# Attention followed by routed experts: separate expert buffers, moved transposes, a later row table and filler matmuls

## The chip, the cores and the metric

The kernel runs on one core of one Trainium2 chip. The metric is the device time of one execution in microseconds (us); three runs of the kernel before gave 316.18, 316.77 and 318.23. The core has five engines that this text names: TensorE (PE in the profile, PEld for its weight loads), VectorE (DVE), ScalarE (ACT), GpSimd (POOL) and SyncE (SP). They run at the same time and wait for each other by semaphores. TensorE writes only to PSUM, the accumulation memory[...].

## What is computed

Block-wise causal attention for 8 batches, 8 heads, 576 tokens and 64 values a head, followed by a mixture of 8 experts. A token's expert is found from its id alone.

```python
scores = scale * q @ k.T                      # 576 x 576 for each batch and head
mask   = block_i >= block_j                   # blocks of 64 tokens
attn   = exp(where(mask, scores, -1e9) - max); attn /= sum(attn)
x      = (attn @ v) -> rows (4608, 512)       # one row for each token
expert = token_ids * 2654435761 % 8           # the factor is 1 modulo 8, so: the low three bits of the id
for e in range(8):
    out[expert == e] = relu(x[expert == e] @ w1[e]) @ w2[e]   # 512 -> 1024 -> 512
```

## The kernel before

The kernel has two stages. **Attention** works through 32 pairs of heads (4 pairs a batch), numbered g = 0 to 31. For one pair, three chunks of scores (`S_chunk`) are computed into PSUM tiles of pool `psS`, of which there are two; ScalarE takes the exp of each chunk into `pt`. The outputs (`PV`) of a pair are computed one turn later, into the single PSUM tile `O`, and VectorE divides by the row sums (`norm`) into `xs`. After each batch, `xs` is written to a table of rows in device memory, `x_dram`.

Queries and keys arrive with tokens on the partitions and must be transposed first. `T_group(b, n)` is a quarter of that for batch b: 18 transposes on TensorE into one PSUM tile, and one VectorE copy into `qT` or `kT`.

```python
def S_chunk(g, ch):
    ps = psS.tile([P, 2, 512], F32, tag="ps")            # two buffers
    for n, (o0, kt, q0, w) in enumerate(CHUNKS[ch]):
        mm_pair(b, pr, ps, o0, kt, q0, w, first=n == 0)   # L172
    for o0 in MASKS[ch]:
        mm_mask(ps, o0, ...)                              # L182
    nc.scalar.activation(ptv[...], ps[:], ACT.Exp, scale=SCALE)   # L200

def T_group(b, n, pool=None):
    if b not in qkTs:
        qkTs[b] = [att.tile([P, NP, S], BF16, name=x, tag=x, bufs=3) for x in ("qT", "kT")]
    ...
    for c in range(n):
        for m in range(2):
            nc.tensor.transpose(...)                      # L159
    copy(qkTs[b][w]..., tp[...])                          # L164, VectorE
```

Beside this, VectorE, GpSimd and TensorE build the **row table**: which token stands in which slot of which expert. `route()` computes the slots in steps (`next(rgen)` runs the next step), and `place_a`, `place_p`, `place_b`, `place_c` enter one batch at a time: comparisons on VectorE (L387, L391), products on GpSimd, five matmuls on TensorE (L411), an addition on VectorE. `placed` ends it.

The turn of one pair, with the lists that say what goes where:

```python
for n in range(WARM):                                     # WARM = 40
    nc.tensor.matmul(warm[:, 0, 0:P], ...)
rgen = route(); next(rgen)
load_qk(0); load_v(0); load_qk(1); load_v(1)
T_group(0, 2); T_group(0, 3, pool=(psO, "O")); T_group(0, 0, pool=(psS, "ps")); T_group(0, 1, pool=(psS, "ps"))

for g in range(NPAIRS + 1):
    S_chunk(g, 0); S_chunk(g, 1)
    for bn in Ts[g, 0]: T_group(*bn)       # between scores and outputs
    if g >= 1:
        PV(g - 1, 0); PV(g - 1, 1)          # L237, L242
        if g in mids: pq = place_b(mids[g], g - 1)
        norm(g - 1)                         # L254, L255
        if g in mids: place_c(pq)
    S_chunk(g, 2)
    if pr == 0: S_rest(b)                   # a small fourth chunk, once a batch
    for bn in Ts[g, 1]: T_group(*bn)       # behind the third chunk
    for step in steps[g]: step()
    ...                                     # write_x, gathers, loads
att_ctx.close()                             # the attention pools end here
mx = ctx.enter_context(tc.tile_pool(name="mx", bufs=2))   # xT and hT of the experts
```

The **expert stage** gathers the rows of an expert from `x_dram` (128 rows a tile, `gather_x`, L463, on GpSimd), transposes them on TensorE (L561) with a copy to `xT` by VectorE (L562), multiplies by w1 with a relu on ScalarE into `hT` (L574, L579; for the first two experts in parts, L593, L597), multiplies by w2 (L607) and scatters the rows to the output (L614). The first three tiles of experts 0 and 1 are gathered already during attention, since they hold only rows of batches 0 to 5.

Of the kernel before, what the change touches and what calls it, by code (L numbers as in the profile page):

```python
# [10 lines left out]
F32 = mybir.dt.float32  # L11
BF16 = mybir.dt.bfloat16
# [7 lines left out]
B, H, S, D = 8, 8, 576, 64  # L20
RUN = 18
DV = 96
NV = 4
E, DM, FF = 8, 512, 1024
N = B * S
NT = 4
NP = H // 2
# [4 lines left out]
GA = EARLY // 128  # L32
OVT = 32
NG = E * G + OVT
WARM = 40
NEG = -30000.0
SCALE = 1.0 / float(D) ** 0.5

# [2 lines left out]
def kernel(  # L41
# [10 lines left out]
    nc = tc.nc  # L52
    P = nc.NUM_PARTITIONS

    const = ctx.enter_context(tc.tile_pool(name="const", bufs=1))
    dram = ctx.enter_context(tc.tile_pool(name="dram", bufs=1, space=bass.MemoryType.DRAM))
    wts = ctx.enter_context(tc.tile_pool(name="wts", bufs=2))

    x_dram = dram.tile([N, DM], BF16, name="x_dram")

# [6 lines left out]
    onesbf = const.tile([P, P], BF16, name="onesbf")  # L67
# [5 lines left out]
    inc = const.tile([P, E], F32, name="inc")  # L73

    nc.vector.memset(onesbf[:], 1.0)
    nc.gpsimd.iota(jmp[:], pattern=[[1, P]], base=0, channel_multiplier=-1,
                   allow_small_or_imprecise_dtypes=True)
    nc.vector.tensor_single_scalar(identbf[:], jmp[:], 0.0, op=ALU.is_equal)
    nc.vector.tensor_single_scalar(lower[:], jmp[:], 0.0, op=ALU.is_gt)

    nc.vector.memset(maskk[:], 0.0)
    nc.vector.memset(maskq[:], 0.0)
    for m in range(2):
# [4 lines left out]
    psS = att_ctx.enter_context(tc.tile_pool(name="psS", bufs=2, space=bass.MemoryType.PSUM))  # L88
    psT = att_ctx.enter_context(tc.tile_pool(name="psT", bufs=1, space=bass.MemoryType.PSUM))
    psO = att_ctx.enter_context(tc.tile_pool(name="psO", bufs=1, space=bass.MemoryType.PSUM))  # L90
    ld = att_ctx.enter_context(tc.tile_pool(name="ld", bufs=2))
    fix = att_ctx.enter_context(tc.tile_pool(name="fix", bufs=1))
    att = att_ctx.enter_context(tc.tile_pool(name="att", bufs=2))
# [53 lines left out]
    qkTs = {}  # L147


    def T_group(b, n, pool=None):  # L150
        if b not in qkTs:
            qkTs[b] = [att.tile([P, NP, S], BF16, name=x, tag=x, bufs=3) for x in ("qT", "kT")]
        w, z = divmod(n, 2)
        c0, n = RUN // 2 * z, RUN // 2
        pool, tag = pool or (psT, "tp")
        tp = pool.tile([P, 16, P], BF16, name="tp", tag=tag)
        for c in range(n):
            for m in range(2):
                nc.tensor.transpose(out=tp[64 * m : 64 * m + 64, c, :],  # L159
                                    in_=loaded[b][w][:, m, c0 + c, :], identity=identbf[:])  # L160
        parts = ((nc.vector.tensor_copy, 0, P),) if b > 0 else (
            (nc.vector.tensor_copy, 0, 64), (nc.scalar.copy, 64, P))
        for copy, r0, r1 in parts:
            copy(qkTs[b][w][:].rearrange("p r (j c) -> p (r j) c", c=RUN)[:, r0:r1, c0 : c0 + n],  # L164
                 tp[:, 0:n, r0:r1].rearrange("p c r -> p r c"))
# [25 lines left out]
    def S_chunk(g, ch):  # L191
        b, pr = divmod(g, NP)
        ps = psS.tile([P, 2, 512], F32, name="ps", tag="ps")
# [3 lines that stand above are left out]
            mm_mask(ps, o0, last=o0 == MASKS[ch][-1])  # L197
        pt = pts[g % 2]
        ptv = pt[:, 0 : 2 * PTW].rearrange("p (m n) -> p m n", m=2)
        nc.scalar.activation(ptv[:, :, 512 * ch : 512 * ch + 512], ps[:], ACT.Exp, scale=SCALE)  # L200

    def S_rest(b):
        qT, kT = qkTs[b]
        ps = psS.tile([P, 2, 512], F32, name="ps", tag="ps")
        for pr in range(NP):
            for m in range(2):
                rows = slice(64 * m, 64 * m + 64)
                nc.tensor.matmul(
                    ps[rows, 0, 64 * pr : 64 * pr + 64],
                    lhsT=kT[rows, pr, 512:576], rhs=qT[rows, pr, 512:576],  # L210
                    start=(pr == 0), stop=(pr == NP - 1),
                )
        nc.scalar.activation(pt4s[b % 2][:, 0 : NP * 64], ps[:, 0, 0 : NP * 64], ACT.Exp, scale=SCALE)
# [63 lines left out]
    def route():  # L277
# [2 lines left out]
        nc.vector.tensor_single_scalar(ei[:], lo[:, :, 0], E - 1, op=ALU.bitwise_and)  # L280
        eb = rt.tile([B, S], BF16, name="eb")
        nc.vector.tensor_copy(eb[:], ei[:])
        pr = psT.tile([P, 5, 65], F32, name="pr", tag="tp")
        for i in range(5):
            n = P if i < NT else 64
            nc.tensor.matmul(pr[0:n, i, 0:B], lhsT=eb[:, 128 * i : 128 * i + n],
                             rhs=identbf[0:B, 0:B], start=True, stop=True)
# [59 lines left out]
        for z, sl in ((0, slice(0, 5 * BA)), (1, slice(5 * BA, T))):  # L347
            n = sl.stop - sl.start
# [35 lines left out]
    def place_a(b):  # L384
        ohp = rt.tile([P, 5, P], BF16, name="ohp", tag="ohp", bufs=2)
        ohg = rt.tile([P, 5, 2, NG], BF16, name="ohg", tag="ohg", bufs=2)
        nc.vector.tensor_tensor(  # L387
            out=ohp[:], in0=iota_p[:, None, :].to_broadcast([P, 5, P]),
            in1=slo[:, b, :, None].to_broadcast([P, 5, P]), op=ALU.is_equal)
        ohs = rt.tile([P, 5, NG], BF16, name="ohs", tag="ohs", bufs=2)  # L390
        nc.vector.tensor_tensor(  # L391
            out=ohs[:], in0=iota_p[:, None, 0:NG].to_broadcast([P, 5, NG]),
            in1=shi[:, b, :, None].to_broadcast([P, 5, NG]), op=ALU.is_equal)
        places[b] = (ohp, ohg, ohs)

    def place_p(b):
        ohp, ohg, ohs = places[b]
        nc.gpsimd.tensor_tensor(
            out=ohg[:, :, 0, :], in0=ohs[:],
            in1=vhi[:, b, :, None].to_broadcast([P, 5, NG]), op=ALU.mult)  # L400
        nc.gpsimd.tensor_tensor(
            out=ohg[:, :, 1, :], in0=ohs[:],
            in1=vlo[:, :, None].to_broadcast([P, 5, NG]), op=ALU.mult)


    def place_b(b, g):
        ohp, ohg, _ = places.pop(b)
        pq = ots[g][:, 0, 512 - 2 * NG :]
        for i in range(5):
            n = P if i < NT else 64  # L410
            nc.tensor.matmul(pq, lhsT=ohp[0:n, i, :],  # L411
                             rhs=ohg[0:n, i, :, :].rearrange("p w g -> p (w g)"),
                             start=(i == 0), stop=(i == 4))
        return pq
# [60 lines left out]
    rgen = route()  # L475
# [3 lines left out]
    load_qk(1)  # L479
    load_v(1)  # L480
    T_group(0, 2)
    T_group(0, 3, pool=(psO, "O"))
    T_group(0, 0, pool=(psS, "ps"))
    T_group(0, 1, pool=(psS, "ps"))

    Ts = {(g, z): [] for g in range(NPAIRS + 1) for z in range(2)}
    for b in range(1, B):
        at = {1: ((1, 1), (2, 0), (2, 1), (3, 0)), 2: ((4, 1), (5, 1), (6, 0), (6, 1))}.get(
            b, tuple((4 * b - 5 + z, 1) for z in range(4)))
        for n, gz in zip((2, 3, 0, 1), at):  # L490
            Ts[gz].append((b, n))
    steps = {g: [] for g in range(NPAIRS + 1)}
# [3 lines left out]
    steps[4] += [lambda: next(rgen, None), rows]  # L496
    mids = {}
    for j in range(B):
        steps[5 + 2 * j].append(lambda j=j: place_a(j))
        steps[6 + 2 * j].insert(0, lambda j=j: place_p(j))  # L500
        mids[9 + 2 * j] = j
    steps[24].append(placed)
    loads = {g: [] for g in range(NPAIRS + 1)}
    for b, g in enumerate((1, 4, 7, 10, 13, 16), 2):
        loads[g].append((load_qk, b))
        loads[g + 1 if b > 2 else 3].append((load_v, b))
    for g, what in ((19, (load_w1, 0)), (21, (load_w1, 1)), (22, (load_w2, 0)), (29, (load_w2, 1))):
        loads[g].append(what)
    for g in range(NPAIRS + 1):
        b, pr = divmod(g, NP)  # L510
        live = g < NPAIRS
        if live:
            S_chunk(g, 0)
            S_chunk(g, 1)
        for bn in Ts[g, 0]:
            T_group(*bn)
        if g >= 1:
            PV(g - 1, 0)
            PV(g - 1, 1)
            if g in mids:  # L520
                pq = place_b(mids[g], g - 1)
            norm(g - 1)
            if g in mids:
                place_c(pq)
        if live:
            S_chunk(g, 2)
            if pr == 0:
                S_rest(b)
        for bn in Ts[g, 1]:
            T_group(*bn)  # L530
        for step in steps[g]:
            step()
        if pr == 0 and b >= 1:
            write_x(b - 1)
        if 12 <= g < 12 + 2 * G:
            nc.gpsimd.memset(xgs[g - 12][:], 0.0)
        if g in (28, 29):
            gather_x(g - 28, 0, GA)
        for load, n in loads[g]:
            load(n)  # L540
    att_ctx.close()


    mx = ctx.enter_context(tc.tile_pool(name="mx", bufs=2))
    mo = ctx.enter_context(tc.tile_pool(name="mo", bufs=8))
    psH = ctx.enter_context(tc.tile_pool(name="psH", bufs=2, space=bass.MemoryType.PSUM))
    psY = ctx.enter_context(tc.tile_pool(name="psY", bufs=2, space=bass.MemoryType.PSUM))
# [110 lines left out]
    with tc.For_i(0, n_ov, 1) as j:  # L658
# [16 lines left out]
        tp = psY.tile([P, NKT, P], BF16, name="tp", tag="yp")  # L675
# [4 lines left out]
        for ft in range(NFT):  # L680
            hp = psY.tile([P, P], F32, name="hpo", tag="yp")
            for db in range(NKT):
                nc.tensor.matmul(hp[:], lhsT=w1b[:, db, ft::NFT], rhs=xt[:, db, :],
                                 start=(db == 0), stop=(db == NKT - 1))
            nc.scalar.activation(ht[:, ft, :], hp[:], ACT.Relu)
        yp = psY.tile([P, DM], F32, name="ypo", tag="yp")
        for ft in range(NFT):
            nc.tensor.matmul(yp[:], lhsT=ht[:, ft, :], rhs=w2b[:, ft, :],
                             start=(ft == 0), stop=(ft == NFT - 1))
# [36 lines left out]
```

The softmax here doesn't subtract the row's maximum and nothing guards it: scores larger than these inputs give would overflow.

## Time and profile before

The profiled execution has a span of 314.1 us.

| Engine | busy, us | share of the span |
|---|---|---|
| TensorE, matmuls | 262.8 | 84% |
| TensorE, weight loads | 197.2 | 63% |
| GpSimd | 168.9 | 54% |
| ScalarE | 144.4 | 46% |
| VectorE | 139.7 | 44% |

The three largest groups: the exps of attention on ScalarE (L200), 96 of 1024 ns each, 93.1 us; the second matmuls of the experts on TensorE (L607), 70.2 us; the first matmuls of the experts (L574), 53.3 us. The shares are averages over two stages. The first exp starts at 13.34 us, the normalisation of the last pair ends at 134.95 us, and the first expert matmul starts at 141.06 us.

How to read the lines below: a line of a timeline has the start in us, the duration in us, the engine, the line of the program, the operation, written tile <- read tiles, the shape, and a count where equal instructions were merged. Square brackets hold the time that the engine stood idle before it, and what released it. The clock is TensorE's granted clock as a share of full speed.

### The profile page before, as it was taken

The page shows a single profiled execution, that of the slowest core. Times are in us where ns is not written, and L with a number is a line of the kernel's source. Part 1 is how long each engine was busy: PE and PEld are TensorE (multiplying, and loading weights), DVE is VectorE, ACT ScalarE, POOL GpSimd, SP SyncE. Part 2 cuts the span into 40 slices and gives each one's busy share as a digit, 9 for nine tenths or more (in the row PEclk, how much of TensorE's full clock was granted, in tenths as well). Part 3 has the DMA queues.
Part 4 walks back from the last instruction along what each step waited for, and adds up shares of the span by engine and source line. Part 5 has one row for each costly group of instructions (what it writes and reads, how often), then busy time and mean ns, then how long its engine had stood idle before and what let it go on. Part 6 is the DMA issues. An engine that isn't in the chain of part 4 may idle for free. (4 is left out here: it accounts for less than half of the span.)

```text
span 314.1 us, 7645 instructions
## 1 busy us (share of the span) xinstructions
PE 262.8 (84%) x3255; PEld 197.2 (63%) x3255; DVE 139.7 (44%) x263; ACT 144.4 (46%) x173; POOL 168.9 (54%) x217
## 2 busy tenths in 40 slices
PE   5687699998989874629889899989999899999960
PEld 5566577776767753426576594865948659486420
DVE  6657988997997831220111404123141240411430
ACT  1676859998989985404243060330603306033000
POOL 8865968889691117137065752745837451241650
PEclk9769989999999999658799999999999999999996
DMA  6997999999999914823049995595895968155330
GB/s 102 182 185 144 175 184 227 180 198 198 214 208 227 218 52 157 155 79 87 14 78 222 229 210 184 141 214 216 147 249 152 213 218 172 48 140 119 123 148 2
DMA packets 53571, 50.36 MB, mean 160 GB/s; under 512 B 40098, under 2 KB 44004, under 8 KB 51488
## 3 DMA queue, kind: packets, MB, share of 16 engines
q0 software_dynamic: 50480, 46.87, 82.2%
q1 hardware_dynamic: 3056, 2.99, 3.1%
q8 instruction: 26, 0.43, 0.5%
q14 instruction: 9, 0.07, 0.1%
HBM read 67.15 MB, written 15.20 MB: 262 GB/s over the span
## 5 line engine op out<-in xcount | busy, mean ns | idle before, releaser
L200 ACT ACTIVATE pt<-ps 128x1024 bf16<-128x1024 f32 x96 | 93.1, 1024 | 23.6 <-PE ps L182 17.7
L614 POOL DMA_INDIRECT out_dram<-ysb,perm x40 | 39.7, 994 | 64.2 <-DVE ysb L612 59.4
L579 ACT ACTIVATE hT<-hp 128x640 bf16<-128x640 f32 x48 | 33.8, 704 | 84.7 <-PE hp L574 82.3
L607 PE MATMUL yp<-w2b,hT 128*128 128x512 bf16 x320 | 70.2, 379 | 0.0
L463 POOL DMA_INDIRECT xg<-x_dram,perm x40 | 40.8, 1021 | 24.4 <-issue 13.2
L607 PEld LDWEIGHTS <-hT 128*128 128x128 bf16 x320 | 31.1, 98 | 36.1
L574 PE MATMUL hp<-xT,w1b 128*128 128x320 bf16 x384 | 53.3, 299 | 0.4 <-DVE xT L562 0.4
L574 PEld LDWEIGHTS <-w1b 128*128 128x128 bf16 x384 | 52.2, 144 | 1.5 <-issue 0.5
L612 DVE COPY ysb<-yp 128x512 f32<-128x512 f32 x40 | 27.7, 692 | 55.6 <-PE yp L607 53.6
L172 PE MATMUL ps<-qT,kT 64*128 64x512 bf16 (+4 forms) x320 | 38.5, 306 | 16.1 <-ACT pt L200 14.7
L562 DVE COPY xT<-tpx 128x512 bf16<-128x512 bf16 x40 | 15.5, 421 | 66.2 <-PE tpx L561 60.3
L237 PE MATMUL O<-vx,pt 128*128 128x65 bf16 x896 | 37.5, 200 | 2.1 <-issue 1.3
L237 PEld LDWEIGHTS <-pt 128*128 128x128 bf16 x896 | 33.0, 102 | 4.7 <-issue 1.8
L172 PEld LDWEIGHTS <-kT 64*128 64x128 bf16 x320 | 14.5, 95 | 26.4 <-issue 18.4
L124 POOL DMA_DIRECT2D vx<-in_v_dram x32 | 28.5, 907 | 3.0 <-DMA vx<-in_v_dram 2.1
L255 DVE TENSOR_TENSOR xs<-O,rs 128x640 bf16<-128x640 f32 x32 | 26.4, 825 | 1.1
L593 PE MATMUL hp<-xT,w1b 128*128 128x384 bf16 (+1 forms) x128 | 21.6, 333 | 2.3 <-DVE xT L562 2.3
L561 PE MATMUL tpx<-identbf,xg 128*128 128x128 bf16 x160 | 14.1, 225 | 11.1 <-DVE xT L562 8.6
L597 ACT ACTIVATE hT<-hp 128x768 bf16<-128x768 f32 (+1 forms) x16 | 11.3, 704 | 24.7 <-PE hp L593 24.1
L164 DVE COPY kT<-tp 128x1152 bf16<-128x1152 bf16 (+1 forms) x16 | 20.5, 1281 | 2.9 <-PE tp L159 2.9
L182 PE MATMUL ps<-maskq,maskk 64*128 64x64 bf16 x256 | 21.3, 193 | 0.3 <-issue 0.3
L164 DVE COPY qT<-tp 128x1152 bf16<-128x1152 bf16 (+1 forms) x16 | 20.5, 1281 | 1.8 <-PE tp L159 1.6
(107 smaller groups left out, 231.6 us busy)
## 6 DMA issues: line engine op xcount, KB each, us to landing
w1b<-in_moe_w_dram POOLq DMA_DIRECT2D x8, 1024.0 KB
w2b<-in_moe_w_dram POOLq DMA_DIRECT2D x8, 1024.0 KB
vx<-in_v_dram POOLq DMA_DIRECT2D x32, 128.0 KB
kb<-in_k_dram POOLq DMA_DIRECT2D x7, 576.0 KB
qb<-in_q_dram POOLq DMA_DIRECT2D x7, 576.0 KB
x_dram<-xs SPq DMA_DIRECT2D x5, 512.0 KB, 7.4
x_dram<-xs POOLq DMA_DIRECT2D x3, 512.0 KB
xg<-x_dram,perm POOLq DMA_INDIRECT x40
```

The source lines that it names most:

```text
L124: nc.gpsimd.dma_start(vx[:, :, i, 0:D], v[b, :, 128 * i : 128 * i + 128, :].rearrange("h p d -> p h d"))
L164: copy(qkTs[b][w][:].rearrange("p r (j c) -> p (r j) c", c=RUN)[:, r0:r1, c0 : c0 + n], tp[:, 0:n, r0:r1].rearrange("p c r -> p r c"))
L172: nc.tensor.matmul(ps[:, m, o0 : o0 + n], lhsT=kT[rows, pr, 128 * kt : 128 * kt + 128], rhs=qT[rows, pr, q0 : q0 + n], start=first, stop=F ...
L200: nc.scalar.activation(ptv[:, :, 512 * ch : 512 * ch + 512], ps[:], ACT.Exp, scale=SCALE)
L237: nc.tensor.matmul(O[:, t, :], lhsT=pt[:, m * PTW + o0 : m * PTW + o0 + 128], rhs=vx[:, h, i, 0 : D + 1], start=(n == 0), stop=(n == t),)
L255: nc.vector.tensor_tensor(out=xs[:].rearrange("p t (m r d) -> p r m t d", m=2, r=NP)[:, pr], in0=O[:, :, :, 0:D], in1=rs[:].to_broadcast([ ...
L463: nc.gpsimd.indirect_dma_start(out=xgs[g % (2 * G)][:], out_offset=None, in_=x_dram[0:n, :], in_offset=bass.IndirectOffsetOnAxis(ap=perm3[ ...
L574: nc.tensor.matmul(hp[:, t, 0:HC], lhsT=w1b[:, db, ft::NFT], rhs=xT[:, db, t * HC : (t + 1) * HC], start=(db == 0), stop=(db == NKT - 1),)
L579: nc.scalar.activation(hT[:, ft, :].rearrange("p (t n) -> p t n", t=2), hp[:, :, 0:HC], ACT.Relu)
L607: nc.tensor.matmul(yp[:], lhsT=hT[:, ft, tt * P : (tt + 1) * P], rhs=w2b[:, ft, :], start=(ft == 0), stop=(ft == NFT - 1),)
L612: nc.vector.tensor_copy(ysb[:], yp[:])
L614: ins = nc.gpsimd.indirect_dma_start(out=out[:, :], out_offset=bass.IndirectOffsetOnAxis(ap=perm3[:, gg : gg + 1], axis=0), in_=ysb[:], in ...
```

## The change

It has four purposes.

1. The pool `mx`, with the expert tiles `xT` and `hT`, is opened before the attention pools, so that it has memory of its own rather than memory that attention used. To make room, the V buffers go from four to three and those of `qT` and `kT` from three to two, and the loads of queries, keys and V move to the pairs after which a buffer is free.
2. The transposes of batches 3 to 7 move from behind the third chunk to between the second chunk and the outputs, and one pair later; three of the four groups of batch 2 stand there as well.
3. The row table is entered three pairs later (`place_a`, `place_p`) and ended two pairs later (`place_b`, `placed`), and the routing matmuls at the start go behind two transpose groups and into another PSUM tile.
4. Fillers: ten more warm-up matmuls, and eleven matmuls on constant data in the first pair, whose results nobody reads, to keep TensorE busy.

```diff
-NV = 4
+NV = 3
-WARM = 40
+WARM = 50
+    mx = ctx.enter_context(tc.tile_pool(name="mx", bufs=2))      # before the attention pools
 ...
-            qkTs[b] = [att.tile([P, NP, S], BF16, name=x, tag=x, bufs=3) for x in ("qT", "kT")]
+            qkTs[b] = [att.tile([P, NP, S], BF16, name=x, tag=x) for x in ("qT", "kT")]     # pool att: 2
 ...
         nc.vector.tensor_copy(eb[:], ei[:])
-        pr = psT.tile([P, 5, 65], F32, name="pr", tag="tp")
+        yield
+        pr = psS.tile([P, 5, 65], F32, name="pr", tag="ps")
 ...
+    def fill(n):
+        if not fills:
+            fills[0] = psO.tile([P, 2, 512], F32, name="fill", tag="O")
+        for _ in range(n):
+            nc.tensor.matmul(fills[0][:, 0, 0 : 3 * P], lhsT=onesbf[:], rhs=ones3[:], start=True, stop=True)
 ...
     T_group(0, 2)
     T_group(0, 3, pool=(psO, "O"))
+    next(rgen)
     T_group(0, 0, pool=(psS, "ps"))
     T_group(0, 1, pool=(psS, "ps"))
 ...
-        at = {1: ((1, 1), (2, 0), (2, 1), (3, 0)), 2: ((4, 1), (5, 1), (6, 0), (6, 1))}.get(
-            b, tuple((4 * b - 5 + z, 1) for z in range(4)))
+        at = {1: ((1, 1), (2, 0), (2, 1), (3, 0)), 2: ((4, 1), (5, 0), (6, 0), (7, 0))}.get(
+            b, tuple((4 * b - 4 + z, 0) for z in range(4)))
 ...
-        steps[5 + 2 * j].append(lambda j=j: place_a(j))
-        steps[6 + 2 * j].insert(0, lambda j=j: place_p(j))
-        mids[9 + 2 * j] = j
-    steps[24].append(placed)
+        steps[8 + 2 * j].append(lambda j=j: place_a(j))
+        steps[9 + 2 * j].insert(0, lambda j=j: place_p(j))
+        mids[11 + 2 * j] = j
+    steps[26].append(placed)
 ...
-    for b, g in enumerate((1, 4, 7, 10, 13, 16), 2):
-        loads[g].append((load_qk, b))
-        loads[g + 1 if b > 2 else 3].append((load_v, b))
+    for b, g0, g1 in ((2, 1, 1), (3, 3, 5), (4, 7, 8), (5, 10, 12), (6, 13, 16), (7, 17, 20)):
+        loads[g0].append((load_qk, b))
+        loads[g1].append((load_v, b))
 ...
             S_chunk(g, 0)
             S_chunk(g, 1)
+        if g == 0:
+            fill(4)
 ...
             S_chunk(g, 2)
+            if g == 0:
+                fill(3)
             if pr == 0:
                 S_rest(b)
+            if g == 0:
+                fill(4)
 ...
     att_ctx.close()
-    mx = ctx.enter_context(tc.tile_pool(name="mx", bufs=2))
```

In `Ts`, a key (g, 0) is the place between scores and outputs of turn g, and (g, 1) the place behind its third chunk.

More of the change, by code (lines that the diff above doesn't have):

```diff
@@ L75 @@
     nc.vector.memset(onesbf[:], 1.0)
+    ones3 = const.tile([P, 3 * P], BF16, name="ones3")
     nc.gpsimd.iota(jmp[:], pattern=[[1, P]], base=0, channel_multiplier=-1,
@@ L79 @@
     nc.vector.tensor_single_scalar(lower[:], jmp[:], 0.0, op=ALU.is_gt)
+    nc.vector.memset(ones3[:], 1.0)
     nc.vector.memset(maskk[:], 0.0)
@@ L403, in place_p @@
             in1=vlo[:, :, None].to_broadcast([P, 5, NG]), op=ALU.mult)
+    fills = {}
+    def fill(n):
[3 more added lines that the diff above has]
+            nc.tensor.matmul(fills[0][:, 0, 0 : 3 * P], lhsT=onesbf[:], rhs=ones3[:], start=True, stop=True)
     def place_b(b, g):
```

## The prediction

> **What bounds the kernel now.** The page first: two rows of its forty slices show where each engine works and at what clock.
>
> ```profile
> ACT  1676859998989985404243060330603306033000
> PEclk9769989999999999658799999999999999999996
> ```
>
> One slice is 314.1 / 40 = 7.85 us. ScalarE is full to about slice 15 (120 us): attention. From slice 20 (157 us) TensorE is, in the expert stage. TensorE's clock sags at slices 1 and 2, at 5, and from 16 to 19 (counted from 0). The chain of waits on the page is 0.3% of the span and carries nothing here, so I read the timeline, stage by stage.
>
> Pairs of heads first. TensorE's timeline over one plain pair (start, duration, operation):
>
> ```profile
> 66.32 0.39 PE L172 MATMUL ps<-qT,kT 64*128 64x448 bf16 x4 [0.21 <-ACT pt L200]
> ...
> 66.68 0.60 PE L237 MATMUL O<-vx,pt 128*128 128x65 bf16 x14
> ...
> 67.70 0.39 PE L172 MATMUL ps<-qT,kT 64*128 64x320 bf16 x4
> ...
> 68.08 0.69 PE L159 MATMUL tp<-identbf,qb 128*64 128x128 bf16 x18
> 68.71 0.39 PE L172 MATMUL ps<-qT,kT 64*128 64x512 bf16 x2
> ...
> 69.33 0.39 PE L172 MATMUL ps<-qT,kT 64*128 64x448 bf16 x4 [0.20 <-ACT pt L200]
> ```
>
> A pair is 69.33 - 66.32 = 3.01 us. Two score tiles (psS) go round, so the second score chunk waits for the exp of the last pair's third chunk. From there a closed loop runs: second chunk to outputs 0.36, outputs to third chunk 1.02, third chunk to its exp 0.55 (74.79 to 75.34), that exp 1.02, release 0.07: 3.02. Three exps in a row take 2.86, so the **loop**, not ScalarE's work alone, sets the pair. The transposes (68.08 to 68.71: 0.63) lie outside it today: they run while ScalarE works, and TensorE still waits 0.20 afterwards.
>
> What the same transposes cost inside the loop is already in this trace. Batch 1 has two of its groups between scores and outputs. Pair 3, on TensorE and on ScalarE:
>
> ```profile
> 25.64 0.39 PE L172 MATMUL ps<-qT,kT 64*128 64x448 bf16 x4
> ...
> 26.75 0.69 PE L159 MATMUL tp<-identbf,qb 128*64 128x128 bf16 x18 [0.69 <-DVE qT L164]
> 27.38 0.60 PE L237 MATMUL O<-vx,pt 128*128 128x65 bf16 x14
> ```
>
> ```profile
> 24.56 3.03 ACT L200 ACTIVATE pt<-ps 128x1024 bf16<-128x1024 f32 x3 [1.02 <-PE ps L182]
> 28.95 2.86 ACT L200 ACTIVATE pt<-ps 128x1024 bf16<-128x1024 f32 x3 [1.36 <-PE ps L182]
> ```
>
> ScalarE sits idle 1.36 us. Taking away the 0.69 that the group itself waited for a copy leaves 0.67: the 0.63 of transposes, nearly whole.
>
> The largest hole in attention, on both engines:
>
> ```profile
> 38.90 1.17 PE L159 MATMUL tp<-identbf,qb 128*64 128x128 bf16 x18 [2.02 <-DVE kT L164]
> ```
>
> ```profile
> 42.45 7.03 ACT L200 ACTIVATE pt<-ps 128x1024 bf16<-128x1024 f32 x7 [4.21 <-PE ps L182]
> ```
>
> VectorE was late because the row table's last step (34.11 to 36.70) and the first place_a (38.76 to 40.03) stood among its copies.
>
> Last the seam between the stages, all engines:
>
> ```profile
> 134.13 0.82 DVE L255 TENSOR_TENSOR xs<-O,rs 128x640 bf16<-128x640 f32 x1
> ...
> 135.10 1.01 PE L561 MATMUL tpx<-identbf,xg 128*128 128x128 bf16 x8 [1.26 <-DVE xs L255]
> 135.26 0.81 POOL L263 DMA_DIRECT2D x_dram<-xs  x1 [8.81 <-DVE xs L255]
> ...
> 139.49 0.76 DVE L562 COPY xT<-tpx 128x512 bf16<-128x512 bf16 x2 [4.53 <-DMA x_dram<-xs]
> ...
> 141.06 7.02 PE L593 MATMUL hp<-xT,w1b 128*128 128x384 bf16 x32 [0.51 <-DVE xT L562]
> ```
>
> The transposed expert rows are in PSUM at 136.1, but their copy waits until 139.49 for the write of xs to land. No data links the two; the new tile takes over memory of the closed attention pools.
>
> **What the skill says.** "TensorE: Matmul & The Clock Gate", section "Step-by-step: what each phase is for": matmuls stay in program order, only weight loads are pulled ahead. The trace agrees: in pair 3 the outputs stood behind the late transposes until 27.38. Same page, "What's actually happening": the array is at half rate until a window of about 3.4 us has been busy, and falls back after an idle one. The trace agrees in kind: the granted clock is 0.50 from 15 to 21 us and from 8 to 11, and 1.00 from 42 to 122. "Perfetto Trace Analysis", section "Optimization Strategy" under "Identifying Performance Opportunities": a repeated bubble on the engine that should be full can mean too few buffers. That is the 0.20 us wait above, for one of two score tiles.
>
> **The change, part by part.**
>
> Start. First exp at 13.34. The query transposes wait for their load at 9.63 and 11.13, so moving the routing matmuls behind two transpose groups, and ten more warm-up matmuls, do not move it. The fillers are 11 matmuls of 384 columns, about 11 x 0.17 = 1.9 us at full clock (21 weight loads of L593, one for each matmul of 384 columns, take 3.52 us from 144.22), in TensorE's gaps between 13.9 and 16.3. If they hold the clock, the outputs of pair 0 take 1.0 instead of 1.8 us (17.32 to 19.09) and some of the idle 0.96 and 0.73 of ScalarE goes: **-1.4 us**, an estimate.
>
> Row table later. VectorE keeps the step at 34.11 but loses place_a from pairs 5 to 7. Following its queue with the same durations, the group of pair 5 is copied by about 36.4 and that of pair 6 goes at once: ScalarE's hole in pair 6 becomes about 1.0 instead of 4.21: **-3.2 us**. The other placements, eight times about 0.35 on TensorE, only shift.
>
> Transposes. Before, batch 1 has two groups between scores and outputs and batch 2 one (pair 6). After, batch 2 has three (pairs 5, 6, 7) and batches 3 to 7 four each (pairs 8 to 27): 22 more pairs with 0.63 us inside the loop. VectorE keeps up: a pair with copy, place_a and normalising takes it 3.44 (66.11 to 69.55), under 3.64. **22 x 0.63 = +13.9 us.**
>
> Buffers. Three V buffers and two qT/kT instead of four and three: every load stands after the pair that frees its buffer, each V eight pairs or more ahead of its first use. **0.**
>
> Expert buffers of their own. The first copy no longer waits: the rows are copied at about 135.8 instead of 139.49, **-3.7 us**. The second expert's copies start at 149.46 although their transposes end near 148.5, and its matmuls run cold until 154.7; at half rate those 3.9 us cost about 1.9. With a shorter wait some of 0.9 + 1.9 goes too; I choose **-1.8**. The late gathers still wait for the write (139.51 before), but they are needed only some 10 us later. The expert stage behind follows the earlier start: from 200 to 300 us TensorE is busy for at least 94% of every 20 us, so nothing else has to be waited for.
>
> Sum: -1.4 - 3.2 + 13.9 - 3.7 - 1.8 = +3.8 us.
>
> One thing stays unexplained. Between 122.6 and 126.9 ScalarE, VectorE and TensorE all stand still, released by what the trace calls "remote", while GpSimd issues gathers; then TensorE is cold to 134. It costs about 5 us, and neither program nor data explains it. I give it one chance in three to be absent from a shifted program: -1.6. Together +2.2: 316.8 + 2.2 = **319.0 us**.
>
> **Rivals.** First: the transposes cost nothing where they are put, because TensorE was about to wait anyway. For it: TensorE has 0.2 us free a pair, and a shorter run to the next scores. Against it: that wait stands before the second chunk, not behind it, and pair 3 shows the bubble. Then the sum loses 13.9 and the time is about 305. Second: the loop hides a part, or VectorE, with the copy now ahead of normalising, holds the outputs (one O tile), and each pair costs 0.4 to 0.9: 314 to 325. Third: the seam gives nothing, because the rows' write, the gathers behind it and the cold clock set the start of the expert matmuls instead. For it: gathers wait until 139.51. Against it: the first three gathers of both experts are issued by 125.8. Then about 324.
>
> **Range and chances.** The seam and the hole in pair 6 are read off single waits and should hold within 2 us. The loop's 13.9 rests on 22 repeats of one measured bubble; the clock and the unexplained pause add some 4 us either way. That gives 310 to 326. Two per cent are 310.4 and 323.1. Faster by over 2% needs the first rival or two lucky clocks: 0.12. Slower by over 2% needs the loop in full and a poor seam: 0.21. Within: 0.67.
>
> **What would show it.** In the changed trace: from pair 8 to 27 second-chunk starts about 3.64 us apart in plain pairs, and an idle ScalarE of about 0.65 before each third exp; no 4.21 hole; the expert copies starting within 1 us of their transposes, with no wait for the write of xs; the granted clock above 0.9 between 15 and 21 us; attention ending some 8 to 10 us later than 134.95. I am wrong if those bubbles are missing (then far faster), or if the expert stage waits for gathers or weights.

## The result and the profile after

The changed kernel takes 324.96 us (median of 4 runs, 324.30 to 326.02), beside 316.48 for the kernel before in the same group of runs: a ratio of 1.026, with a 95% interval of 1.021 to 1.031. It is slower by 8.5 us.

Six instants, read from the timelines of the two profiled executions, show where the time went. "Third exp" is the exp of a pair's third chunk of scores.

| Instant, us from the start | before | after | difference | change since the line above |
|---|---|---|---|---|
| first exp starts | 13.34 | 21.09 | +7.75 | +7.75 |
| third exp of pair 8 starts | 48.46 | 55.52 | +7.06 | -0.69 |
| third exp of pair 27 starts | 112.58 | 128.55 | +15.97 | +8.91 |
| last pair normalised | 134.95 | 150.93 | +15.98 | +0.01 |
| first expert matmul starts | 141.06 | 153.29 | +12.23 | -3.75 |
| end of the span | 314.1 | 322.3 | +8.2 | -4.03 |

There are two losses, of about 8 and 9 us, and a gain of 7.8 us at the seam and behind it. The first loss is new. The changed kernel's timeline, all engines, around its first pair:

```profile
16.96 1.27 POOL L130 DMA_DIRECT2D v<-in_v_dram  x2
18.20 0.19 POOL L299 IOTA iota_e<- 128x8 f32 x1
...
18.42 0.49 DVE L302 TENSOR_TENSOR oh<-et,iota_e 128x320 f32<-128x320 f32 x1 [9.25 <-POOL iota_e L299]
18.83 1.42 DVE L167 COPY qT<-tp 128x576 bf16<-128x576 bf16 x2
19.62 1.38 ACT L167 COPY qT<-tp 128x576 bf16<-128x576 bf16 x2 [10.12 <-DVE qT L167]
...
20.39 0.61 PE L175 MATMUL ps<-qT,kT 64*128 64x512 bf16 x2 [8.98 <-ACT qT L167]
```

VectorE stands still for 9.25 us before a comparison of the routing step, because one of its inputs, a row of eight indices, is made on GpSimd, and GpSimd's queue now has all loads of batches 0 and 1 ahead of it. The copies of the queries stand behind that comparison, and the first scores behind the copies. The queries were transposed long before.

The second loss, TensorE's timeline of a plain pair after the change, and ScalarE's line for it:

```profile
60.79 0.40 PE L175 MATMUL ps<-qT,kT 64*128 64x448 bf16 x4 [1.23 <-ACT pt L203]
...
61.14 0.69 PE L162 MATMUL tp<-identbf,qb 128*64 128x128 bf16 x18
61.77 0.60 PE L240 MATMUL O<-vx,pt 128*128 128x65 bf16 x14
...
62.79 0.39 PE L175 MATMUL ps<-qT,kT 64*128 64x320 bf16 x4
...
64.42 0.40 PE L175 MATMUL ps<-qT,kT 64*128 64x448 bf16 x4 [0.93 <-ACT pt L203]
```

```profile
63.34 2.86 ACT L203 ACTIVATE pt<-ps 128x1024 bf16<-128x1024 f32 x3 [0.77 <-PE ps L185]
```

The pair takes 64.42 - 60.79 = 3.63 us instead of 3.01; the transposes (61.14 to 61.77, 0.63) stand between the second chunk and the outputs. ScalarE idles 0.77 us ahead of the third exp, and TensorE's own wait, 0.20 before, is 0.93: both engines now wait for each other.

The seam, all engines:

```profile
150.11 0.82 DVE L258 TENSOR_TENSOR xs<-O,rs 128x640 bf16<-128x640 f32 x1
...
151.08 1.69 PE L580 MATMUL tpx<-identbf,xg 128*128 128x128 bf16 x12 [1.26 <-DVE xs L258]
151.23 0.80 POOL L266 DMA_DIRECT2D x_dram<-xs  x1 [8.84 <-DVE xs L258]
151.71 0.85 DVE L581 COPY xT<-tpx 128x512 bf16<-128x512 bf16 x2 [0.77 <-PE tpx L580]
...
153.29 6.42 PE L612 MATMUL hp<-xT,w1b 128*128 128x384 bf16 x32 [0.52 <-DVE xT L581]
```

The copy follows its transposes and no longer waits for the write of xs. The standstill of three engines is there as before, ScalarE's part 4.53 us in both traces:

```profile
142.93 2.86 ACT L203 ACTIVATE pt<-ps 128x1024 bf16<-128x1024 f32 x3 [4.53 <-remote]
```

### The profile page after: what moved, and what is told of

Same layout as the page of the kernel before. It is cut to its first block, busy times and chain, and to the rows that moved or that the text cites. A ratio compares the mean times of both kernels' runs of the same rounds, so it can differ in the third digit from the quotient of the medians.

```text
span 322.3 us, 7677 instructions
## 1 busy us (share of the span) xinstructions
PE 257.9 (80%) x3276; PEld 194.0 (60%) x3276; DVE 139.0 (43%) x260; ACT 143.6 (45%) x173; POOL 168.1 (52%) x217
## 5 line engine op out<-in xcount | busy, mean ns | idle before, releaser
L175 PE MATMUL ps<-qT,kT 64*128 64x512 bf16 (+4 forms) x320 | 36.4, 302 | 38.9 <-ACT pt L203 29.6
L593 PEld LDWEIGHTS <-w1b 128*128 128x128 bf16 x384 | 52.2, 144 | 1.5 <-issue 0.5
L476 POOL DMA_INDIRECT xg<-x_dram,perm x40 | 40.7, 1019 | 17.6 <-issue 9.7
L240 PE MATMUL O<-vx,pt 128*128 128x65 bf16 x896 | 35.4, 197 | 0.8 <-DVE xs L258 0.5
L240 PEld LDWEIGHTS <-pt 128*128 128x128 bf16 x896 | 31.4, 100 | 3.7 <-DVE xs L258 0.7
L612 PE MATMUL hp<-xT,w1b 128*128 128x384 bf16 (+1 forms) x128 | 19.3, 311 | 2.3 <-DVE xT L581 2.3
L612 PEld LDWEIGHTS <-w1b 128*128 128x128 bf16 x128 | 16.2, 145 | 5.0 <-DVE xT L581 2.2
```

The lines of the kernel that those rows point to most:

```text
L175: nc.tensor.matmul(ps[:, m, o0 : o0 + n], lhsT=kT[rows, pr, 128 * kt : 128 * kt + 128], rhs=qT[rows, pr, q0 : q0 + n], start=first, stop=F ...
L240: nc.tensor.matmul(O[:, t, :], lhsT=pt[:, m * PTW + o0 : m * PTW + o0 + 128], rhs=vx[:, h, i, 0 : D + 1], start=(n == 0), stop=(n == t),)
L476: nc.gpsimd.indirect_dma_start(out=xgs[g % (2 * G)][:], out_offset=None, in_=x_dram[0:n, :], in_offset=bass.IndirectOffsetOnAxis(ap=perm3[ ...
L593: nc.tensor.matmul(hp[:, t, 0:HC], lhsT=w1b[:, db, ft::NFT], rhs=xT[:, db, t * HC : (t + 1) * HC], start=(db == 0), stop=(db == NKT - 1),)
L612: nc.tensor.matmul(hp[:, ft - f0, 0 : P * (t1 - t0)], lhsT=w1b[:, db, ft::NFT], rhs=xT[:, db, c], start=(db == 0), stop=(db == NKT - 1),)
```

## The experiments

There were twelve runs in three groups. All kernels of a group ran on the same chip beside the kernel before, which took 316.95, 310.27 and 311.24 us in the three groups; so only ratios within a group are compared. The standstill is in all traces of the first group and in none of the other two. "Both repairs" means the index row made first and the transposes back at their old places.

**The index row first** (first group).

```diff
     def route():
+        iota_e = rt.tile([P, E], F32, name="iota_e")
+        nc.gpsimd.iota(iota_e[:], ...)
         lo = tid[:].bitcast(I32)...
 ...                                      # and gone from behind the yield
```

> Changed kernel with one instruction group moved: the small index row iota_e of the routing is made ahead of the first loads instead of behind them on GpSimd. Theory (the start): VectorE no longer stands 9.25 us before the one-hot comparison, the query copies behind it follow at once, first exp near 12.5 us instead of 21.09; the clock then holds in the first pairs, so 8 to 9.5 us less: 315.5 to 317. Rival (the late start is bound by the query loads or by GpSimd's queue as well, and the rest of the loss is the transposes): less than 3 us gained, 322 or more.

Measured: 1.010 (1.004 to 1.017), 320.21 us. ScalarE's first line of the pairs:

```profile
13.66 1.94 ACT L203 ACTIVATE pt<-ps 128x1024 bf16<-128x1024 f32 x2
```

The first exp is back at 13.66, and the last pair is normalised at 143.61 instead of 150.93, 7.3 us earlier. The cause of the late start is shown. The time fell by less than the 8 to 9.5 us expected, by 1.6% or 5 us. A part of the difference stands in the trace: the experts' first partial matmuls took 7.83 us, where they took 6.42 in the changed kernel's, since the clock stayed at half until 5.0 us after their start rather than 2.2 us. Why it came back later was not tested.

**The transposes at their old places** (first group).

```diff
-2: ((4, 1), (5, 0), (6, 0), (7, 0))}.get(b, tuple((4 * b - 4 + z, 0) for z in range(4)))
+2: ((4, 1), (5, 1), (6, 0), (6, 1))}.get(b, tuple((4 * b - 5 + z, 1) for z in range(4)))
```

> Changed kernel with the transposes of batches 2 to 7 back behind the third chunk, one pair earlier, still with two qT/kT buffers. Theory (loop): a batch of four pairs falls from 15.4 to 13.2-13.7 us, 22 pairs with 0.45 each: 10 us less, 315. Rival 1 (the full 0.63 each): 14 us less, 311. Rival 2 (the transposes cost nothing where they are, the late start is all): no gain within 1 us.

Measured: 1.006 (1.002 to 1.009), 317.96 us; the last pair is normalised at 141.92, 9.0 us earlier than in the changed kernel. Over 22 pairs that is 0.4 us each, near the 0.45 of the loop theory, but it is a net figure. An undisturbed batch of this run takes 12.90 us, where the changed kernel takes 15.4: 0.62 a pair, nearly the full length of the transposes. The rest is single stalls that this run has and the changed kernel has not: ScalarE stands idle 2.79 us in pair 6 again, and one batch takes 14.26 us.

**Both repairs** (first group, and again in the third).

> Both of the two repairs above together. If start and transposes are independent, the gains add: 325 - 8.5 - 10 = 306 to 307, some 3% under the kernel before. If one hides the other (VectorE's queue being full again behind the third chunk, as in the hole of pair 6 before), about 311.

> The kernel with both repairs once more, beside the others of this group, since its first four times spread over 6 us and its variants gained 3.2 to 3.5% in another group. If the standstill of 4.6 us shows in its trace, 0.975 to 0.985 of the kernel before; if it does not, 0.965 to 0.97.

Measured: 0.986 (0.977 to 0.994) at first, with four times from 308 to 315 us, so less was gained than the 3% expected; in the third group 0.966 (0.962 to 0.969), 300.48 us. In the first group's trace the last pair is normalised at 133.37, which is 17.6 us earlier than in the changed kernel; alone the repairs gave 7.3 and 9.0. In attention they add up, and a little more. The second trace has no standstill, as expected for that ratio.

**The transposes alone, in the kernel before** (second group), with its three qT/kT buffers, its row table and its start.

> The kernel before, with one part of the change alone: the transposes of batches 2 to 7 between scores and outputs, one pair later. Theory (loop): a batch of four pairs in the middle goes from 13.4 to 15.4 us, with 0.6 us of idle ScalarE ahead of each third exp of pairs 2 and 3 of a batch, attention ends about 9 us later, 324 to 327. Rival (a part of it came from the other parts of the change: the placements, the fewer buffers): 320 or less.

Measured: 1.027 (1.023 to 1.032), 317.98 us beside 310.27. The direction and the loop are as the theory has them, in this kernel too. ScalarE's lines in pairs 5 to 8:

```profile
36.56 2.86 ACT L200 ACTIVATE pt<-ps 128x1024 bf16<-128x1024 f32 x3 [0.95 <-PE ps L182]
40.37 2.85 ACT L200 ACTIVATE pt<-ps 128x1024 bf16<-128x1024 f32 x3 [0.96 <-PE ps L182]
44.00 2.85 ACT L200 ACTIVATE pt<-ps 128x1024 bf16<-128x1024 f32 x3 [0.77 <-PE ps L182]
47.63 1.02 ACT L200 ACTIVATE pt<-ps 128x1024 bf16<-128x1024 f32 x1 [0.77 <-PE ps L182]
```

The hole of 4.21 us in pair 6 is gone here although the row table is where it was, so the moved transposes closed it. The next run closes it too, without the wait in every pair. It is the later pair, or the copy's new place ahead of the normalising, that closes the hole, and not the loop.

**The transposes between the first and the second chunk** (third group). The changed kernel with the index row first:

```diff
             S_chunk(g, 0)
+        for bn in Ts[g, 0]:
+            if g > 3:
+                T_group(*bn)
+        if live:
             S_chunk(g, 1)
 ...
         for bn in Ts[g, 0]:
-            T_group(*bn)
+            if g <= 3:
+                T_group(*bn)
```

> The changed kernel with the index row first, and the transposes of batches 2 to 7 at their new pairs but ahead of the second chunk rather than behind it, where TensorE waits for ScalarE anyway. Theory (loop): outside the loop they cost nothing, a batch of four pairs takes 13.0 to 13.5 us rather than 15.4, and the time is within 1% of that with both repairs. Rival (it is the later pair, or VectorE's copy ahead of normalising, that costs): 15.4 us a batch, 2 to 2.7% slower than with both repairs.

Measured: 0.962 (0.957 to 0.967), 300.04 us; with both repairs 0.966. TensorE's timeline:

```profile
68.31 0.69 PE L162 MATMUL tp<-identbf,qb 128*64 128x128 bf16 x18
69.13 0.40 PE L175 MATMUL ps<-qT,kT 64*128 64x448 bf16 x4
...
69.49 0.60 PE L240 MATMUL O<-vx,pt 128*128 128x65 bf16 x14
```

The transposes (68.31 to 69.00) now end before the second chunk may start, and the outputs follow it after 0.36 us. Their pairs are the late ones of the change, and the copy still stands ahead of the normalising on VectorE; only the place against the loop differs. A batch takes 13.6 us (the first exps behind two successive fourth chunks start at 62.36 and 75.96), against 15.4. This settles that the loop is what costs.

The batch is still 0.7 us longer than an undisturbed one with both repairs (12.90). All of that stands in one pair of four, the one behind the small fourth chunk: its third exp comes 4.29 us after the last (60.76 to 65.05), where it took 3.59. The other three take what they take with both repairs. In that one pair TensorE's wait stands before the first chunk, not before the second:

```profile
61.84 0.39 PE L175 MATMUL ps<-qT,kT 64*128 64x512 bf16 x2 [0.94 <-ACT pt L203]
...
62.19 0.69 PE L162 MATMUL tp<-identbf,kb 128*64 128x128 bf16 x18
62.82 0.39 PE L175 MATMUL ps<-qT,kT 64*128 64x448 bf16 x4
```

So the transposes push back the second chunk there. The whole time is the same as with both repairs, within the intervals, because this run has no hole in pair 6: from pair 4 to pair 8 it is 2.5 us faster, from pair 8 to pair 27 2.1 us slower.

**The expert tiles after attention again** (first and third group), with both repairs.

```diff
-    mx = ctx.enter_context(tc.tile_pool(name="mx", bufs=2))      # ahead of the attention pools
 ...
     att_ctx.close()
+    mx = ctx.enter_context(tc.tile_pool(name="mx", bufs=2))
```

> Both repairs, but the expert tiles again opened after the attention pools (sharing their memory), as in the kernel before. Theory (the seam): the first expert copies wait again for the write of xs, 3.7 us at the first copy and about 7.8 us by the end (4 from shorter cold spells and the second expert): 314 to 315. Rival (only the wait itself): 310.5. Rival (the seam gives nothing in the end): as with both repairs.

> Both repairs, the expert tiles opened after the attention pools. Theory (the seam waits for the write of xs, and that write stands behind the last weight load when attention ends soon after its issue): where the standstill is missing from the trace, the first copy waits about 9 us and the kernel is 8 to 10 us slower than with both repairs; where it is there, 4 us of wait and 3 to 6 us slower. Rival (only the 3.7 us of the prediction, whatever the load): 3 to 4 us slower in both cases.

Measured: 0.993 (0.990 to 0.996) in the first group, where both repairs had 0.986 with an interval that overlaps it, so the seam's size stayed open there; and 0.993 (0.990 to 0.995) in the third, beside 0.966. There the seam is worth 0.0268 x 311.24 = 8.3 us. The timeline of the third group's run:

```profile
126.80 0.82 DVE L257 TENSOR_TENSOR xs<-O,rs 128x640 bf16<-128x640 f32 x1
...
127.92 0.80 POOL L265 DMA_DIRECT2D x_dram<-xs  x1 [2.01 <-DVE xs L257]
...
136.66 0.75 DVE L581 COPY xT<-tpx 128x512 bf16<-128x512 bf16 x2 [9.04 <-DMA x_dram<-xs]
```

The wait is 9.04 us, not 4.53: without the standstill attention ends some 2 us after the last weight load was issued, and the write of xs lands 8.7 us after its issue instead of 4.2 in the kernel before. (The load was issued at 125.30 here and attention ended at 127.62; in the kernel before it was 125.83 and 134.95.) The run with the transposes alone, also without the standstill, shows the same wait, 9.05 us. With tiles of their own (both repairs, third group) the same write is as late, but only the late gathers wait for it:

```profile
128.60 0.76 DVE L581 COPY xT<-tpx 128x512 bf16<-128x512 bf16 x2 [0.57 <-PE tpx L580]
...
130.18 6.48 PE L612 MATMUL hp<-xT,w1b 128*128 128x384 bf16 x32 [0.52 <-DVE xT L581]
...
136.97 1.07 POOL L476 DMA_INDIRECT xg<-x_dram,perm  x1 [7.31 <-DMA x_dram<-xs]
```

That the weight load ahead of it makes the write late is inferred from the order; the load was not moved to try it.

**The buffers alone** (third group). The kernel before with the expert tiles ahead, three V and two qT/kT buffers and the new load pairs; everything else as before, no fillers.

> The kernel before with the buffers' part alone: expert tiles of their own, three V and two qT/kT buffers, the new load pairs; transposes, row table, routing start as before, no fillers. Theory (seam): 8 to 10 us faster where the standstill is missing, 5 to 6 where it shows, and equal to both repairs within 1%, so that the rest of the change gives nothing. Rival (fewer buffers cost something in attention): attention ends later than in the kernel before by over 1 us.

Measured: 0.963 (0.959 to 0.967), 300.18 us, 11 us faster than the kernel before. That is all of the gain that any run here has: with both repairs it is 0.966, and the intervals overlap, so the later row table, the moved routing step and the fillers add nothing that can be seen. About 8.3 of the 11 us are the expert tiles' own memory, by the run before this one. The fewer buffers cost attention nothing over 1 us: the third exp of pair 27 starts at 113.12, and in the trace of the kernel before at 112.58, though that trace is of another chip.

**The fillers away** (second group): both repairs, no fillers, 40 warm-up matmuls.

> Both repairs, without the eleven fillers and with 40 warm-up matmuls. Theory A (the fillers pay by their clock): the clock stays at half until 21 us as before, the third exp of pair 3 starts 1.4 us later than with them (after first exp: 17.0 instead of 15.65), about 1 us slower. Theory B (they cost what they save, since they run at half clock and push back the third chunk by 0.85): 15.6 again, no difference above 0.5 us.

Measured: 0.968 (0.964 to 0.973), beside 0.965 and 0.969 for the two kernels of the same group that have the fillers. In time the fillers make no difference that can be seen. In the traces their effect is small. From the first exp to the third exp of pair 3:

| Traces | clock, mean from 15 to 21 us | stretch, us |
|---|---|---|
| without fillers, four traces (kernel before, transposes alone, buffers alone, this run) | 0.50 | 15.61 in each |
| with fillers, 50 warm-up matmuls and the index row first, eight traces | 0.73 to 0.88, one 1.00 | 15.04 to 15.85, one 14.52 |

So the clock does come back earlier with the fillers, but the stretch gets shorter by 0.3 us in the mean, not by 1.4. In seven of the eight traces the first fillers themselves run at half clock ahead of the third chunk and push it back; in the eighth the clock was full before they began, and they took little more than half as long. The fillers of both repairs (third group), and of the run that follows next:

```profile
14.44 1.46 PE L416 MATMUL fill<-ones,onesbf 128*128 128x384 bf16 x4
```

```profile
13.52 0.82 PE L416 MATMUL fill<-ones,onesbf 128*128 128x384 bf16 x4
```

**The row table at its old pairs** (second group): both repairs, `place_a` from pair 5 again.

> Both repairs, with the row table entered at the pairs of the kernel before (three pairs earlier). Theory: only the hole of pair 6 changes; ScalarE idles 4.2 us there instead of 2.6, so 1.6 us slower than with both repairs. Rival (moving the table freed VectorE in the later pairs too): more than 3 us slower.

Measured: 0.965 (0.961 to 0.969), no slower than with the later table. ScalarE's hole in pair 6 is 4.59 us here, and 4.21 and 4.27 in the two other traces with the old table and the old transposes. With the later table and the old transposes it is 2.61 to 4.77 in seven traces. In the three of these where the clock is full around the hole it is 2.61, 2.79 and 3.00; in all other traces named here a stretch of half clock falls into it. So a benefit of the later table is not shown.

**The early gathers spread out** (second group), one a pair in pairs 26 to 31.

> Both repairs, with the six early gathers issued one a pair in pairs 26 to 31 instead of three each in pairs 28 and 29. It asks about the stretch of 4.5 us in pair 29 and 30 where three engines stand still. Theory A (it belongs to GpSimd's run of gathers and the weight load behind it): the stretch goes or moves, up to 5 us less and no cold clock behind it. Theory B (it belongs to the place in TensorE's program): it stays between the same matmuls, 4.5 us long.

Measured: 0.969 (0.963 to 0.975). This run can't answer its question. The standstill is missing from its trace, but also from those of the other three kernels of the group, whose gathers were not touched. What it is stays open. It goes with the group, each of which ran on a chip of its own: the kernel with both repairs shows it in the first group's trace and not in the third's. Whether the gathers have a part in it isn't known.

## Why the prediction was right or wrong

The time, 324.96, lies within 310 to 326, near its upper end, and in part by luck. A slowdown of over 2% was given a chance of 0.21, and was to come from "the loop in full and a poor seam". It came instead from a late start that no term of the sum and no rival contained, while the pairs lost less on balance than forecast and the seam gave more. Term by term, in the traces of the two kernels:

| Step | predicted | measured |
|---|---|---|
| Start: routing step moved, warm-up, fillers | -1.4 | +7.75 |
| Pairs up to 8: hole of pair 6, and three of the moved groups | -3.2 + 3 x 0.63 = -1.3 | -0.7 |
| Loop, the other 19 groups | +12.0 | +8.9 |
| Seam | -3.7 - 1.8 = -5.5 | -3.75 - 4.03 = -7.8 |
| Standstill absent | -1.6 | 0 |
| Sum | +2.2 | +8.2 |

**The start is the step that failed.** "Moving the routing matmuls behind two transpose groups ... do not move it" looked at TensorE alone. The routing step also holds work for VectorE and GpSimd, and it moved behind the load issues in GpSimd's order. In the kernel before its row of indices ran at 1.22 us, before the first load; after, at 18.20. With that one instruction ahead of the loads the first exp is at 13.66. Because of the late start the granted clock is 0.50 from 15 to 21 us, where the prediction named over 0.9 as a sign, and attention ends 16 us later instead of 8 to 10. The fillers, the other half of this step, do bring the clock back earlier once the pairs run on time, but the pairs gain 0.3 us from it in the mean, not 1.4.

**The loop was right as a mechanism, and its size in each pair too.** Three kernels show it: moving only the transposes into it costs 2.7%, taking them out again ends attention 9.0 us earlier, and on the other side of the second chunk they are free in three pairs of four. Times from third exp to third exp in one batch, in us:

| Trace | pair 12 to 13 | 13 to 14 | 14 to 15 | 15 to 16 | sum |
|---|---|---|---|---|---|
| before | 3.59 | 3.00 | 3.32 | 3.77 | 13.68 |
| both repairs, third group | 3.59 | 3.00 | 3.31 | 3.00 | 12.90 |
| after | 4.21 | 3.62 | 3.94 | 3.62 | 15.39 |

Against the undisturbed batch in the middle row, each pair of the changed kernel is longer by 0.62 to 0.63. What the sum of +12.0 missed is the 3.77 in the first row: the kernel before lost time to single stalls, and the changed kernel has none between pairs 8 and 27. Undisturbed, those 19 steps of the kernel before would take some 61.2 us, an estimate from the steps of the middle row's trace; they took 64.12, and 73.02 after. So the loop cost 11.8 us, 0.62 a pair, and 2.9 us of stalls went away. Three of them are TensorE standing idle in the middle of its own work, 0.59, 0.52 and 0.41 us, released by nothing that the profile shows. Why the changed kernel has none isn't known.

**The later row table was misread.** It was to shrink the hole of pair 6 to 1.0 us (-3.2). With the table later and the transposes at their old places, the hole is still 2.61 to 4.77. VectorE's lines before show why:

```profile
36.76 0.82 DVE L255 TENSOR_TENSOR xs<-O,rs 128x640 bf16<-128x640 f32 x1
37.50 1.35 DVE L164 COPY kT<-tp 128x1152 bf16<-128x1152 bf16 x1
38.76 0.81 DVE L387 TENSOR_TENSOR ohp<-iota_p,slo 128x640 bf16<-128x640 bf16 x1
```

TensorE's transposes at 38.90 waited for the copy that ran from 37.50 to 38.85. That copy stood behind the table's last step and a normalising; place_a (38.76) came after it and could not delay it. With both repairs (third group) place_a is gone from there, and the copy is no earlier; it ends at 39.23, where the prediction had about 36.4:

```profile
37.14 0.82 DVE L258 TENSOR_TENSOR xs<-O,rs 128x640 bf16<-128x640 f32 x1
37.88 1.35 DVE L167 COPY kT<-tp 128x1152 bf16<-128x1152 bf16 x1
```

```profile
39.28 0.69 PE L162 MATMUL tp<-identbf,qb 128*64 128x128 bf16 x18 [2.52 <-DVE kT L167]
```

The hole did go in the changed kernel, as forecast, but by a cause that the prediction did not name: the moved transposes.

**The seam** was right in its cause. From the end of normalising to the first expert matmul it took 6.11 us before and 2.35 after, so the first part, 3.7, came out at 3.75, and the three other traces of the first group with expert tiles of their own have 2.35 as well. The second part came out at 4.0 instead of 1.8 in this one pair of traces: the second expert's first partial matmuls took 5.42 us, where they took 7.11 before. But from the first expert matmul to the end it is 173.0 us before, 169.1 after, and 170.4 to 171.7 in those three other traces. The second part is thus 1.4 to 4.0 us from trace to trace, and 1.8 is not shown to be wrong. In the kernel before the clock falls to half a second time, from 151.3 to 154.7 us, while the second expert runs; in none of those four traces does it. What the prediction did not see is that the wait can be longer than 4.53: where the standstill is missing it is 9 us, probably because of the weight load issued just ahead.

**The standstill** was there again. From the third exp of pair 27 to that of pair 31 it is 18.6 us in both kernels, and 12.4 with both repairs in the third group, where it is missing. So it costs about 6.2 us, not about 5. The clock behind it stayed at half until 144.5 us in the kernel before, not until 134.

**The rivals.** Transposes that cost nothing at their new place are ruled out, and so is a seam that gives nothing. The second rival, 0.4 to 0.9 a pair because the loop hides a part or VectorE holds the outputs, fits the net 8.9 us over 19 pairs, 0.47 each, but not the mechanism: the loop hid nothing, and with the copy still ahead of the normalising three pairs of four pay nothing once the transposes stand before the second chunk. No rival was a late start.

## What to carry to other kernels

A step moved in the program moves on every engine that it uses: before calling a move free, list the step's instructions on each queue and look at what now stands ahead of them. Where two engines pass tiles to each other through few buffers, the closed loop is the bound, and work is free only at the point of it where its engine waits; here 0.63 us of transposes cost 0.62 us one place further on. When a forecast adds such costs to a measured time, take off the stalls that the measured time already holds: here they were 2.9 us. Tiles that take over memory of a closed stage inherit that stage's last write as a wait, so give the first tiles of the next stage memory of their own: here that was worth 8.3 us of about 311, and with the buffer counts and load places that it needed the kernel was 3.7% faster (0.963).

## What the runs showed of the hardware

Two programs ran in the first group and again in the third (both repairs, with the expert tiles early and late). Both show the standstill of 4.5 to 4.7 us in the first group's trace and neither in the third's, and the kernel before took 317 us in the first group and 310 to 311 in the others. A comparison across groups would have mistaken 6 us of it for an effect. Without the standstill the write of xs landed later after its issue, 8.7 us rather than 4.2, so that with shared memory the saved time came back in part as a longer wait at the seam, 9.04 instead of 4.53 us.
